# Transposing two token tiles with one transfer in a fused attention and token-mixer block

## The chip, the cores and the metric

The kernel runs on one core of a Trainium2 chip. The metric is the device time of one execution in microseconds, as the median over runs. A core has TensorE (PE) for matmuls, VectorE (DVE), ScalarE (ACT) and GpSimd (POOL) for elementwise work, and SyncE (SP), which here issues nearly all DMA transfers, one after the other in its queue.

## The reference

A block with adaptive layer norm, 2,048 tokens of 512 features, in bfloat16. The first half is attention in which each token sees 8 tokens at a distance of 2, with 32 heads of 16; the second half is an MLP over the token axis.

```python
mod = (silu(c) @ w_mod).reshape(1, 6, 1, 512)          # sa, ca, ga, sb, cb, gb
h = layernorm(x) * (1 + ca) + sa
qkv = h @ wqkv                                         # 512 -> 3 x 512, 32 heads of 16
logits = q . k[pos - 2 * w], w = 0..7                  # masked where pos - 2 w < 0
o = softmax(logits / 4) weighted sum of v
x = x + ga * (o @ wo)
h = layernorm(x) * (1 + cb) + sb
u = gelu(einsum('bsd,sf->bdf', layernorm(h), w1) + b1) # contracts the tokens, F = 1792
x = x + gb * (einsum('bdf,fs->bds', u, w2) + b2).T
```

## The kernel before

The 2,048 tokens are 16 tiles of 128. They are worked in five chunks of 2, 4, 4, 4 and 2 tiles (`SIZES`), numbered 0 to 4; chunk 2 has tiles 6 to 9, chunk 3 has 10 to 13, chunk 4 has 14 and 15. Each chunk goes through `build_chunk`:

- layer norm of its tiles: `ln1s` (statistics), `rstd1`, `nb1`, and `n1_T`, which writes the normalized tile T into `h3`, tokens on the partitions;
- a transpose of `h3` into `hT`, features on the partitions. Chunks 0 and 1 do it on TensorE (`tr`, evicted by `hT`). Chunks 2 to 4 (`XDMA`) do it by DMA: `xtT` transposes tile T, 128 tokens by 512 features, into four blocks of 128 by 128. `hT` there is laid out as feature block, then token: block k of tile T lies C columns after block k − 1, where C is the number of tokens of the chunk;
- the projections `qkvC_tj` (t = 0 for q, 1 for k, 2 for v): four matmuls each that read `hT` as the moving operand, up to 512 columns, and accumulate over the four feature blocks; evicted to `q_sb`, `k_f` and `v_sb` by `evC_tj`;
- `vdC_d`, DMA copies of shifted values from `v_sb` into a slot of `vD` (five slots);
- `qk` (VectorE products of q with shifted k into `big`), `red` (TensorE sums them into the logits `psL`), `max`, `sub`, `exp`, `esum`, `rcp`, and `smB`, which scales the weights in `lsb` on VectorE;
- `a2_C_j`, four DMA copies that lay `lsb` out anew as `a2sb`; then `pv` (VectorE products of `a2sb` and `vD` into `big`), `pvacc` (TensorE), `oev`, and the output projection `wo`;
- the second and third layer norms, which write `h3` again for the MLP.

The MLP's first matmuls (`mlp1`) take tokens as they come ready and are mixed into the chunks' work; the second ones (`mlp2`) come at the end, when all `gelu` are done. Products of `w_mod` (`modcol`, `mcols`, `mrowt`, `mrows`, `st_row`, `ld_row`) give the modulation rows; `modcol3` uses the last three loads of `w_mod` (`ld_wmod3` to `ld_wmod5`).

The order of all steps is written out by hand in the string `ORDER`, and every engine works its steps in that order. SyncE's queue is one of these orders. A DMA holds SyncE while it is issued, and the data land later; a step that waits for something holds all that stands behind it on its engine. `hT` has two buffers, so chunk 2 overwrites chunk 0's, chunk 3 chunk 1's, and chunk 4 chunk 2's. A helper records every instruction, so the profile gives line 133 for all of them, and they are told apart by their tiles: `hT<-h` are the transposing DMAs, `psS<-hT,w_qkv` the projections, `a2sb<-lsb` the `a2` copies, `vD<-v_sb` the `vd` copies.

On SyncE the steps stand in this order around the transposes, before the change: `ld_wo1 xt6 ld_wmod5 vd0_1 vd0_0 xt8 xt9 xt7 vd0_2`, the four `a2_0`, `ld_wo3 ld_wo2 xt10 ld_wo0 vd0_3 xt12 xt13 xt11 vd1_2 ld_b2`, the four `a2_1`, `vd1_1 st_row0 vd1_3 xt14 ld_row0 vd1_0 vd2_2 xt15`, and then the `a2_2` among other loads.

Of the kernel before, what the change touches and what calls it, by code (L numbers as in the profile page):

```python
# [182 lines left out]
consts ld_x_1_2 act_table ld_x0 ld_x_1_4 ld_c ld_x_2_8 ld_x1 ident ld_x_2_6 ld_wmod1 ln1s3 halo0 ld_wqkv1 cps
ln1s2 warm2 ld_wqkv0 silu_exp ld_wmod0 ln1s0 ln1s4 ln1s1 ln1s5 rstd1_0 ld_x_4_14 nb1_0 ln1s9 rstd1_1 n1_0 n1_1
silu_dve nb1_1 ld_wqkv2 ln1s8 fill:2:70 tr0_0 n1_2 n1_4 modcols1 ln1s7 hT0_3:a n1_5 n1_3 ld_x_3_10 hT0_2:d a1col
hT0_0:a fill:4:16 tr1_2 wsc1_2:d ld_b1 hT0_1:a wsc1_3:d wsc1_0:a tr1_0 wsc1_1:d ln1s6 hT1_2:a ld_wmod2 qkv0_10
ld_x_3_12 wsc0_0:d rstd1_2 wsc0_1:d qkv0_12 wsc0_2:d hT1_1:a nb1_2 n1_8 n1_9 wsc0_3:d modcols0 hT1_0:d ld_wmod3
hT1_3:a qkv0_00 sab ev0_12:d n1_6 ld_wmod4 qvb0 ln1s14 ld_wo1 qkv0_02 qvb_cp0 ln1s15 ev0_00:a wsc2_2 qvb1
wsc2_0:d qkv1_00 wsc2_3 ev0_10:a ev0_02:d ln1s10 wsc2_1:d qkv1_10 qvb_cp1 qk0_0 ev1_10:a qkv0_22 qk0_1 n1_7
qkv0_20 ln1s13 qk0_2 qkv1_02 xt6 red0_0 ev1_00:a qk0_3 red0_1 red0_2 ev0_22:a ld_wmod5 qkv1_22 qk1_0 ev0_20:a  # L190
qkv1_12 ev1_02:a vd0_1 red0_3 ev1_12:a mask qkv1_11 vd0_0 ln1s11 max0 xt8 qk1_2 qkv1_01 ev1_11:a sub0 qkv1_03
ev1_01:a xt9 exp0 qkv1_13 qk1_1 ev1_03:a xt7 esum0 ev1_13:a qkv1_20 rcp0 vd0_2 ln1s12 qkv1_21 smB0 qk1_3 a2_0_3
modcol2 rstd1_4 qkv1_23 a2_0_0 ev1_22:a a2_0_2 halo_v1:a red1_0 ev1_20:a a2_0_1 red1_1 ln1v10 ln1v12 ln1v11
ln1v13 nb1_4 red1_2 rstd1_3 n1_15 ld_wo3 red1_3 nb1_3 ld_wo2 mcols0 n1_11 n1_10 qkv2_00 max1 ev1_21:a n1_14 xt10
qkv2_02 ev2_00:a pv0_0 qkv2_10 n1_12 ld_wo0 pv0_1 qkv2_11 vd0_3 ev2_10:a ev2_02:a qkv2_12 qk2_0 n1_13 qkv2_01
xt12 ev2_12:a pvacc0_0 ev2_01:a sub1 qk2_2 xt13 qkv2_03 exp1 qkv2_13 xt11 ev2_11:a ev2_03:a qkv2_22 qk2_1
ev2_13:a esum1 ev1_23:a qkv2_21 rcp1 vd1_2 red2_0 smB1 ev2_21:a ld_b2 red2_1 qk2_3 halo_v2:a a2_1_1 red2_2
# [5 lines left out]
ld_w1_0_0 oev1_3:a mrowt1 qkv3_03 mrows1:a x1_0 st_row1 qkv4_00 ev3_03:a vd2_0 ln2q1 qk3_2 pvacc1_0 ev4_02:a
red3_1 pvacc1_1 oev1_0:a qkv3_23:q oev1_1:a qk3_3 ev4_00:a wo3:q ln2q0 wo5:q pv2_2 qkv4_22:q x1_5 ev3_23:a wo2:q
ld_row1 ln2q5 ld_w1_0_896 ln2m0 halo_v3:a wo4:q x1_3 pv2_1 x1_2 red3_2 x1_4 red3_3 ln2q3 qkv3_21:q pv2_3 rstd2_0
qkv4_20 ln2q2 ev3_21:a ev4_22:a vd3_3 pvacc2_1 nb2_0 max3 pvacc2_2 n2_0 warm0 ln2q4 vd3_0 n2_1 ln2m2 sub3 pv2_0
pvacc2_3 oev2_2:a exp3 rstd2_2 esum3 oev2_1:a aff0 pvacc2_0 rcp3 oev2_0:a qkv4_10 oev2_3:a ln2m4 nb2_2 smB3
warm3 n2_2 ev4_10:a ln3s0 wo6 a2_3_0 n2_3 ln3s1 a2_3_1 rstd2_4 wo7 x1_6 vd3_1 aff2 rstd3_0 a2_3_2 biascols wo9:q
ev4_20:a a2_3_3 nb2_4 nb3_0 ln3s3 n2_5 n2_4 vd3_2 warm1 ln3s2 h3_1 h3_0 qkv4_12 aff4 rstd3_2 wo8 x1_7 ld_w2_0
nb3_2 ln3s5 h3_3 h3_2 ln2q6 ln3s4 mlp1_0_6_0 ev4_12:a pv3_0 mlp1_0_3_0 x1_9 rstd3_4 mlp1_0_5_0 x1_8 mlp1_0_0_0  # L210
biascols_cp:a ln2q8 nb3_4 pv3_1 halo_v4:a mlp1_0_2_0 h3_4 vd4_1 h3_5 mlp1_0_1_0 ln2q9 pv3_2 ld_w2_1 mlp1_0_2_4
vd4_2 ln2q7 mlp1_0_0_4 vd4_0 mlp1_0_3_4 park0_0:a mlp1_0_1_4 mlp1_0_5_4:q park0_1:a ln2m6 vd4_3 pv3_3 park0_2:a
pvacc3_0 pvacc3_1 oev3_0:a ld_w1_0_1152 pvacc3_2 oev3_1:a mlp1_0_4_0:q rstd2_6 oev3_2:a qk4_2 pvacc3_3 park0_3:a
mlp1_0_7_0 oev3_3:a nb2_6 qk4_1 n2_6 mlp1_0_6_4 mlp1_0_4_4 n2_8 qk4_0 wo12:q ld_w1_0_1408 n2_7 n2_9 qk4_3 wo10:q
park0_4:a aff6 x1_12 red4_0 wo13:q ld_w2_3 park0_5:a ln2q12 red4_1 red4_2 x1_10 red4_3 wo11:q max4 ln2q10 ln3s9
x1_13 sub4:q mlp1_0_8_0:q exp4 ln3s8 ln2q13 mlp1_0_11_0 esum4 ln3s7 rcp4 mlp1_0_12_0 park0_6:a ln3s6 x1_11
mlp1_0_10_0 smB4 rstd3_6 ln2m12 a2_4_2 mlp1_0_9_0 h3_7 rstd2_12 h3_6 a2_4_3 ln2q11 h3_9 mlp1_0_8_4 ln2m13 a2_4_0
nb2_12 ln2m11 n2_12 mlp1_0_7_4 a2_4_1 ln2m10 h3_8 rstd2_10 ld_w2_4 aff12 mlp1_0_9_4 rstd2_13 rstd2_11 nb2_10
ln3s12 mlp1_0_9_8 mlp1_0_7_8 n2_10 mlp1_0_8_8 nb2_13 pv4_0 park0_7:a mlp1_0_12_4 ld_w1_0_1664 park0_8:a
mlp1_0_11_4 nb2_11 pv4_2 n2_13 mlp1_0_10_4 rstd3_12 pv4_1 park0_9:a mlp1_0_12_8 n2_11 mlp1_0_10_8 pv4_3 inj1_4  # L220
mlp1_0_11_8 ld_w1_1_0 park0_10:a pvacc4_2 ld_w1_1_640 park0_11:a pvacc4_0 nb3_12 aff11 pvacc4_1 h3_12 pvacc4_3
mlp1_0_13_0 aff10 oev4_0:a oev4_2:a aff13 mlp1_0_13_4 ln3s10 wo15 ld_w2_5 ln3s13 rstd3_10 mlp1_0_13_8 wo14 x1_15
rstd3_13 park0_12:a inj1_0 nb3_13 ln2s15 mlp1_1_0_6 nb3_10 x1_14 rstd2_15 mlp1_1_4_6 park0_13:a nb2_15 ln2s14
n2_15 inj1_3 inj1_6 ld_w1_1_896 inj1_5 mlp1_1_6_6 rstd2_14 aff15 h3_10 mlp1_1_3_6 ln3s15 mlp1_1_6_10 ln3s11
mlp1_1_0_10 rstd3_15 inj1_1 mlp1_1_1_6 park1_0:a nb3_15 h3_15 n2_14 rstd3_11 aff14 mlp1_1_5_6 h3_13 ln3s14
mlp1_1_5_10 mlp1_1_1_10 inj1_2 ld_w1_2_0 mlp1_1_2_6 h3_11 rstd3_14 park1_1:a h3_14 mlp1_1_4_10 mlp1_1_3_10
mlp1_1_2_10 mlp1_1_9_10 park1_2:a ld_w1_1_1408 park1_3:d mlp1_1_7_10 padd1_9 park1_4:a park1_5:d mlp1_1_8_10
padd1_7 gelu7 mlp1_1_10_10 park1_6:a mlp1_2_2_11 ld_w1_2_640 padd1_10 mlp1_2_2_14 mlp1_2_0_11 padd2_2
mlp1_2_0_14 ld_w2_7 gelu2 mlp1_2_1_11 padd2_0 mlp1_2_1_14 gelu0 mlp1_1_12_10 padd2_1 gelu10 padd1_8 gelu1
mlp1_2_5_11 gelu8 mlp1_2_5_14 gelu9 mlp1_2_6_11 mlp1_2_3_11 padd2_6 mlp1_2_3_14 ld_w2_9 mlp1_2_4_11 padd2_3  # L230
mlp1_2_4_14 padd1_12 gelu3 mlp1_1_13_10 padd2_4 gelu6 padd2_5 gelu4 mlp1_1_11_10 padd1_13 gelu5 gelu13 mlp2_0_0
padd1_11 gelu12 gelu11 mlp2_0_0b ld_w2_11 mlp2_0_0c fin0_0 mlp2_8_0 ld_w2_15 mlp2_4_0 st_out0_0 ld_w2_2 mlp2_9_0
fin4_0 ld_w2_13 mlp2_1_0 st_out4_0 mlp2_3_0 mlp2_6_0 fin3_0 fin1_0 st_out3_0 mlp2_5_0 st_out1_0 fin5_0 mlp2_7_0
st_out5_0 fin8_0 mlp2_2_0 fin9_0 mlp2_13_0 fin2_0 st_out9_0 st_out8_0 st_out2_0 fin7_0 mlp2_10_0 fin13_0
st_out7_0 fin6_0 mlp2_12_0 st_out6_0 st_out13_0 mlp2_11_0 fin12_0 fin10_0 st_out12_0 mlp2_14_0 st_out10_0
fin11_0 st_out11_0 mlp2_15_0 fin14_0 mlp2_15_1 st_out14_0 fin15_0 mlp2_15_2 fin15_1 st_out15_0 st_out15_1
fin15_2 st_out15_2
"""


# [798 lines left out]
```

## Time and profile before

| | |
|---|---|
| time, median of 3 runs | 206.31 us (206.3 to 206.35) |
| profiled execution, first to last instruction | 204.6 us |
| the run's median less that span | 1.7 us |
| TensorE busy | 194.7 us, 95% of the span |
| VectorE busy | 163.3 us, 80% |
| ScalarE busy | 120.6 us, 59% |
| GpSimd busy | 13.0 us, 6% |
| mean granted TensorE clock | 0.998 |
| transposing DMAs | 10, from 22.2 to 57.0 us |

Times inside the profile count from the span's first instruction. "Busy" counts neither waiting nor the issuing of DMAs; SyncE's issues are shown in its timeline as SPq. A matmul's row has its full latency, so matmuls that follow each other overlap; the rate is read from the distance of their starts. A busy share is an average: the stretches of the execution have different limits.

### The profile page before, as it was taken

The page shows a single profiled execution, that of the slowest core. Times are in us where ns is not written, and L with a number is a line of the kernel's source. Part 1 is how long each engine was busy: PE and PEld are TensorE (multiplying, and loading weights), DVE is VectorE, ACT ScalarE, POOL GpSimd, SP SyncE. Part 2 cuts the span into 40 slices and gives each one's busy share as a digit, 9 for nine tenths or more (in the row PEclk, how much of TensorE's full clock was granted, in tenths as well). Part 3 has the DMA queues.
Part 4 walks back from the last instruction along what each step waited for, and adds up shares of the span by engine and source line. Part 5 has one row for each costly group of instructions (what it writes and reads, how often), then busy time and mean ns, then how long its engine had stood idle before and what let it go on. Part 6 is the DMA issues. An engine that isn't in the chain of part 4 may idle for free.

```text
span 204.6 us, 4223 instructions
## 1 busy us (share of the span) xinstructions
PE 194.7 (95%) x1655; PEld 103.5 (51%) x1655; DVE 163.3 (80%) x260; ACT 120.6 (59%) x283; POOL 13.0 (6%) x36
## 2 busy tenths in 40 slices
PE   3999999999999997989899999999999999999994
PEld 3988554454455553554344445444444444444453
DVE  2899999999999999999999999975473204369365
ACT  2398998994666899989898876683762000000000
POOL 4122001100000001240000000100000000000000
...
GB/s 141 330 380 348 117 239 107 161 98 201 247 186 267 308 234 251 25 272 110 289 200 115 26 157 263 288 131 200 340 304 3 232 88 16 39 77 51 51 82 51
DMA packets 55111, 35.93 MB, mean 176 GB/s; under 512 B 24628, under 2 KB 52404, under 8 KB 55092
## 3 DMA queue, kind: packets, MB, share of 16 engines
...
q10 hardware_dynamic: 8, 0.00, 0.0%
...
## 4 chain that ended last, share of the span: by engine, by line
PE 65%; DVE 20%; issue 5%; DMA 5%; SPq 3%; ACT 2%; DVEq 0%
PE psS L133 62%; DVE big L133 9%; DVE h L133 3%; PE psL L133 3%; SPq L133 3%; DVE st L133 3%; DMA wst<-in_B_w_dram 2%; DMA xx<-in_A_x_dram 2%; ACT h L133 1%; DVE mv L133 1%; DVE m L133 1%; DVE lsb L133 1%; DVE ls L133 0%; DVE nb L133 0%; DVE woq L133 0%
## 5 line engine op out<-in xcount | busy, mean ns | idle before, releaser
L133 PE MATMUL psS<-h,wst 128*128 128x512 bf16 (+1 forms) x254 | 50.7, 379 | 1.2 <-POOL h L133 0.7
L133 PE MATMUL psS<-hT,w_qkv 128*128 128x512 bf16 (+3 forms) x312 | 46.2, 339 | 0.3 <-ACT w_qkv L133 0.3
L133 PEld LDWEIGHTS <-wst 128*128 128x128 bf16 (+1 forms) x356 | 28.7, 98 | 32.2 <-issue 3.2
L133 PEld LDWEIGHTS <-w_qkv 128*128 128x128 bf16 (+1 forms) x354 | 29.5, 111 | 21.3 <-issue 3.2
L133 DVE TENSOR_TENSOR big<-a2sb,vD 128x4096 bf16<-128x4096 bf16 (+1 forms) x20 | 36.9, 1876 | 0.0
L133 DVE TENSOR_TENSOR big<-q_sb,k_f 128x4096 bf16<-128x4096 bf16 (+1 forms) x20 | 36.3, 1857 | 0.0
L133 DVE SCALAR_TENSOR_TENSOR h<-psS,bcol,rows_bc 128x512 f32<-128x512 f32 (+2 forms) x18 | 12.4, 690 | 24.4 <-PE psS L133 24.2
L133 PE MATMUL psS<-gT,big 128*128 128x512 bf16 x112 | 24.8, 379 | 0.0
L133 PEld LDWEIGHTS <-big 128*128 128x128 bf16 x144 | 12.0, 97 | 13.2
L133 PEld LDWEIGHTS <-ident 128*128 128x128 bf16 (+1 forms) x203 | 13.9, 111 | 5.9 <-issue 2.8
L133 PE MATMUL psS<-woq,o_sb 128*32 128x512 bf16 (+1 forms) x172 | 16.6, 380 | 0.0
L133 ACT ACTIVATE h<-xx,nb,rs 128x512 bf16<-128x512 bf16 x19 | 15.0, 807 | 0.8 <-DVE nb L133 0.7
L133 DVE TENSOR_TENSOR psS<-psS,gT 128x512 f32<-128x512 f32 x14 | 9.3, 696 | 7.0 <-PE psS L133 7.0
L133 ACT ACTIVATE junk<-xx 128x512 bf16<-128x512 bf16 x22 | 13.8, 626 | 0.2
L133 POOL TENSOR_SCALAR h<-xx,rs,nb 128x512 bf16<-128x512 bf16 x9 | 7.3, 813 | 101.3 <-DVE nb L133 84.0
L133 ACT ACTIVATE lv<-mv,epscol 128x1 f32<-128x1 f32 (+2 forms) x25 | 7.3, 291 | 9.3 <-DVE mv L133 8.4
L133 DVE BATCH_NORM_STATS2 st<-xx 128x6 f32<-128x512 bf16 x14 | 9.5, 678 | 4.0 <-DMA xx<-in_A_x_dram 4.0
L133 ACT ACTIVATE gT<-psS,bcol 128x512 bf16<-128x512 f32 x14 | 8.7, 688 | 6.4 <-DVE psS L133 6.4
L133 PEld LDWEIGHTS <-group 128*32 128x32 bf16 x288 | 6.8, 96 | 10.2 <-issue 4.8
L133 DVE TENSOR_TENSOR h<-h,rows_bc 128x512 bf16<-128x512 bf16 (+2 forms) x20 | 11.5, 581 | 0.5
L133 DVE TENSOR_TENSOR h<-h,xx 128x512 bf16<-128x512 f32 (+2 forms) x18 | 11.4, 633 | 0.6
L133 ACT ACTIVATE gT<-psS 128x512 bf16<-128x512 f32 x19 | 10.8, 587 | 1.6 <-PE psS L133 1.5
...
## 6 DMA issues: line engine op xcount, KB each, us to landing
...
```

What stands on the lines that cost most here:

```text
L133: r = fn(*a, **k)
```

## The change

A parameter `XG=2` is added. In chunks 2 to 4 one transposing DMA handles two tiles: the source is 128 tokens by 2 x 512 columns of `h3`, and the result is eight blocks of 128 by 128. `hT` of these chunks is now laid out by tile, then feature block, so that the blocks of one transfer follow each other. A projection's moving operand for feature block kt is now one piece of 128 columns from each tile of the chunk, 512 columns apart, instead of one contiguous row. Chunks 0 and 1 stay as they are. Ten transposing DMAs become five: `xt6` (tiles 6 and 7), `xt8` (8 and 9), `xt10`, `xt12` and `xt14`. In `ORDER` they stand where the chunk's last ones stood; nothing else is moved.

```diff
     XDMA=(2, 3, 4),
+    XG=2,
...
+        rhs_of = lambda kt: hT[:, kt, :]
         if ch in XDMA:
-            first = None
-            for sl, st in enumerate(tiles):
-                dma_t = lambda sl=sl, st=st: nc.sync.dma_start_transpose(out=hT[:, :, sl * P:(sl + 1) * P],
-                                                                         in_=h3[:, st, :])
-                add("sp", 1.25, dma_t, reads=[("n1", st)] + ([("hT_raw", bh)] if sl else []),
+            hX = hT_r[bh][:, 0:KT * C].rearrange("p (s k q) -> p s k q", s=nt, k=KT)
+            rhs_of = lambda kt: hX[:, :, kt, :]
+            for sl in range(0, nt, XG):
+                st = t0 + sl
+                dma_t = lambda sl=sl, st=st: nc.sync.dma_start_transpose(
+                    out=hX[:, sl:sl + XG, :, :].rearrange("p s k q -> p (s k) q"),
+                    in_=h3[:, st:st + XG, :].rearrange("p s d -> p (s d)"))
+                add("sp", 1.25, dma_t, reads=[("n1", s) for s in range(st, st + XG)] + ([("hT_raw", bh)] if sl else []),
                     writes=[("hTr", ch, sl)] + ([] if sl else [("hT_raw", bh)]), bytes_=0.95, lat=1.2, desc=8,
                     name=f"xt{st}")
-            hkeys = [("hTr", ch, sl) for sl in range(nt)]
+            hkeys = [("hTr", ch, sl) for sl in range(0, nt, XG)]
...
-                        mm(ps(s_)[:, (j - j0) * C:(j - j0 + 1) * C], lhsT=lhsT, rhs=hT[:, kt, :],
+                        mm(ps(s_)[:, (j - j0) * C:(j - j0 + 1) * C], lhsT=lhsT, rhs=rhs_of(kt),
```

SyncE's order after it: `ld_wo1 ld_wmod5 vd0_1 vd0_0 xt6 xt8 vd0_2`, the four `a2_0`, `ld_wo3 ld_wo2 ld_wo0 vd0_3 xt10 xt12 vd1_2 ld_b2`, the four `a2_1`, `vd1_1 st_row0 vd1_3 ld_row0 vd1_0 vd2_2 xt14`, and the rest as before.

More of the change, by code (lines that the diff above doesn't have):

```diff
@@ L182 @@
 ORDER = """
[L183 to L197, printed above, removed]
@@ L198 @@
-pvacc0_1 a2_1_3 qkv3_00 a2_1_2 qkv3_10 a2_1_0 pv0_2 mrowt0 vd1_1 qkv2_20 ev3_10:a pv0_3 ev3_00:a red2_3 mrows0:a
-qkv2_23 ev2_20:a st_row0 max2 halo_k3:p ev2_22:a vd1_3 qkv3_11 qk3_0 xt14 qkv3_22 ev3_11:a pvacc0_2 ld_row0
-pvacc0_3 sub2:q oev0_2:a vd1_0 pv1_2 qkv3_02:q exp2 qkv3_12 ev3_02:a ev2_23:a qkv3_01 pv1_3 oev0_0:a vd2_2 esum2
-modcol3 xt15 rcp2 ev3_12:a woq_s qkv3_20 ev3_01:a pvacc1_3 smB2 ev3_20:a red3_0 qk3_1 ev3_22:a a2_2_0 pvacc1_2
-wo1 a2_2_1 vd2_3 qkv3_13:q x1_1 a2_2_2 pv1_1 vd2_1 wo0 ev3_13:a a2_2_3 qkv4_02 ld_w1_0_512 oev1_2:a mcols1 pv1_0
@@ L203 @@
[L203 to L237, printed above, removed]
+consts ld_x_1_2 act_table ld_x0 ld_x_1_4 ld_c ld_x_2_8 ld_x1 ident ld_x_2_6 ld_wmod1 ln1s3 halo0 ld_wqkv1 cps ln1s2
@@ new lines @@
+warm2 ld_wqkv0 silu_exp ld_wmod0 ln1s0 ln1s4 ln1s1 ln1s5 rstd1_0 ld_x_4_14 nb1_0 ln1s9 rstd1_1 n1_0 n1_1 silu_dve
+nb1_1 ld_wqkv2 ln1s8 fill:2:70 tr0_0 n1_2 n1_4 modcols1 ln1s7 hT0_3:a n1_5 n1_3 ld_x_3_10 hT0_2:d a1col hT0_0:a
+fill:4:16 tr1_2 wsc1_2:d ld_b1 hT0_1:a wsc1_3:d wsc1_0:a tr1_0 wsc1_1:d ln1s6 hT1_2:a ld_wmod2 qkv0_10 ld_x_3_12
+wsc0_0:d rstd1_2 wsc0_1:d qkv0_12 wsc0_2:d hT1_1:a nb1_2 n1_8 n1_9 wsc0_3:d modcols0 hT1_0:d ld_wmod3 hT1_3:a qkv0_00
+sab ev0_12:d n1_6 ld_wmod4 qvb0 ln1s14 ld_wo1 qkv0_02 qvb_cp0 ln1s15 ev0_00:a wsc2_2 qvb1 wsc2_0:d qkv1_00 wsc2_3
@@ new lines @@
+ev0_10:a ev0_02:d ln1s10 wsc2_1:d qkv1_10 qvb_cp1 qk0_0 ev1_10:a qkv0_22 qk0_1 n1_7 qkv0_20 ln1s13 qk0_2 qkv1_02
+red0_0 ev1_00:a qk0_3 red0_1 red0_2 ev0_22:a ld_wmod5 qkv1_22 qk1_0 ev0_20:a qkv1_12 ev1_02:a vd0_1 red0_3 ev1_12:a
+mask qkv1_11 vd0_0 ln1s11 max0 qk1_2 qkv1_01 ev1_11:a sub0 qkv1_03 ev1_01:a exp0 qkv1_13 qk1_1 ev1_03:a xt6 xt8 esum0
+ev1_13:a qkv1_20 rcp0 vd0_2 ln1s12 qkv1_21 smB0 qk1_3 a2_0_3 modcol2 rstd1_4 qkv1_23 a2_0_0 ev1_22:a a2_0_2 halo_v1:a
+red1_0 ev1_20:a a2_0_1 red1_1 ln1v10 ln1v12 ln1v11 ln1v13 nb1_4 red1_2 rstd1_3 n1_15 ld_wo3 red1_3 nb1_3 ld_wo2 mcols0
@@ new lines @@
+n1_11 n1_10 qkv2_00 max1 ev1_21:a n1_14 qkv2_02 ev2_00:a pv0_0 qkv2_10 n1_12 ld_wo0 pv0_1 qkv2_11 vd0_3 ev2_10:a
+ev2_02:a qkv2_12 qk2_0 n1_13 qkv2_01 ev2_12:a pvacc0_0 ev2_01:a sub1 qk2_2 qkv2_03 exp1 qkv2_13 xt10 xt12 ev2_11:a
+ev2_03:a qkv2_22 qk2_1 ev2_13:a esum1 ev1_23:a qkv2_21 rcp1 vd1_2 red2_0 smB1 ev2_21:a ld_b2 red2_1 qk2_3 halo_v2:a
+a2_1_1 red2_2 pvacc0_1 a2_1_3 qkv3_00 a2_1_2 qkv3_10 a2_1_0 pv0_2 mrowt0 vd1_1 qkv2_20 ev3_10:a pv0_3 ev3_00:a red2_3
+mrows0:a qkv2_23 ev2_20:a st_row0 max2 halo_k3:p ev2_22:a vd1_3 qkv3_11 qk3_0 qkv3_22 ev3_11:a pvacc0_2 ld_row0
@@ new lines @@
+pvacc0_3 sub2:q oev0_2:a vd1_0 pv1_2 qkv3_02:q exp2 qkv3_12 ev3_02:a ev2_23:a qkv3_01 pv1_3 oev0_0:a vd2_2 esum2
+modcol3 xt14 rcp2 ev3_12:a woq_s qkv3_20 ev3_01:a pvacc1_3 smB2 ev3_20:a red3_0 qk3_1 ev3_22:a a2_2_0 pvacc1_2 wo1
+a2_2_1 vd2_3 qkv3_13:q x1_1 a2_2_2 pv1_1 vd2_1 wo0 ev3_13:a a2_2_3 qkv4_02 ld_w1_0_512 oev1_2:a mcols1 pv1_0 ld_w1_0_0
+oev1_3:a mrowt1 qkv3_03 mrows1:a x1_0 st_row1 qkv4_00 ev3_03:a vd2_0 ln2q1 qk3_2 pvacc1_0 ev4_02:a red3_1 pvacc1_1
+oev1_0:a qkv3_23:q oev1_1:a qk3_3 ev4_00:a wo3:q ln2q0 wo5:q pv2_2 qkv4_22:q x1_5 ev3_23:a wo2:q ld_row1 ln2q5
@@ new lines @@
+ld_w1_0_896 ln2m0 halo_v3:a wo4:q x1_3 pv2_1 x1_2 red3_2 x1_4 red3_3 ln2q3 qkv3_21:q pv2_3 rstd2_0 qkv4_20 ln2q2
+ev3_21:a ev4_22:a vd3_3 pvacc2_1 nb2_0 max3 pvacc2_2 n2_0 warm0 ln2q4 vd3_0 n2_1 ln2m2 sub3 pv2_0 pvacc2_3 oev2_2:a
+exp3 rstd2_2 esum3 oev2_1:a aff0 pvacc2_0 rcp3 oev2_0:a qkv4_10 oev2_3:a ln2m4 nb2_2 smB3 warm3 n2_2 ev4_10:a ln3s0
+wo6 a2_3_0 n2_3 ln3s1 a2_3_1 rstd2_4 wo7 x1_6 vd3_1 aff2 rstd3_0 a2_3_2 biascols wo9:q ev4_20:a a2_3_3 nb2_4 nb3_0
+ln3s3 n2_5 n2_4 vd3_2 warm1 ln3s2 h3_1 h3_0 qkv4_12 aff4 rstd3_2 wo8 x1_7 ld_w2_0 nb3_2 ln3s5 h3_3 h3_2 ln2q6 ln3s4
@@ new lines @@
+mlp1_0_6_0 ev4_12:a pv3_0 mlp1_0_3_0 x1_9 rstd3_4 mlp1_0_5_0 x1_8 mlp1_0_0_0 biascols_cp:a ln2q8 nb3_4 pv3_1 halo_v4:a
+mlp1_0_2_0 h3_4 vd4_1 h3_5 mlp1_0_1_0 ln2q9 pv3_2 ld_w2_1 mlp1_0_2_4 vd4_2 ln2q7 mlp1_0_0_4 vd4_0 mlp1_0_3_4 park0_0:a
+mlp1_0_1_4 mlp1_0_5_4:q park0_1:a ln2m6 vd4_3 pv3_3 park0_2:a pvacc3_0 pvacc3_1 oev3_0:a ld_w1_0_1152 pvacc3_2
+oev3_1:a mlp1_0_4_0:q rstd2_6 oev3_2:a qk4_2 pvacc3_3 park0_3:a mlp1_0_7_0 oev3_3:a nb2_6 qk4_1 n2_6 mlp1_0_6_4
+mlp1_0_4_4 n2_8 qk4_0 wo12:q ld_w1_0_1408 n2_7 n2_9 qk4_3 wo10:q park0_4:a aff6 x1_12 red4_0 wo13:q ld_w2_3 park0_5:a
@@ new lines @@
+ln2q12 red4_1 red4_2 x1_10 red4_3 wo11:q max4 ln2q10 ln3s9 x1_13 sub4:q mlp1_0_8_0:q exp4 ln3s8 ln2q13 mlp1_0_11_0
+esum4 ln3s7 rcp4 mlp1_0_12_0 park0_6:a ln3s6 x1_11 mlp1_0_10_0 smB4 rstd3_6 ln2m12 a2_4_2 mlp1_0_9_0 h3_7 rstd2_12
+h3_6 a2_4_3 ln2q11 h3_9 mlp1_0_8_4 ln2m13 a2_4_0 nb2_12 ln2m11 n2_12 mlp1_0_7_4 a2_4_1 ln2m10 h3_8 rstd2_10 ld_w2_4
+aff12 mlp1_0_9_4 rstd2_13 rstd2_11 nb2_10 ln3s12 mlp1_0_9_8 mlp1_0_7_8 n2_10 mlp1_0_8_8 nb2_13 pv4_0 park0_7:a
+mlp1_0_12_4 ld_w1_0_1664 park0_8:a mlp1_0_11_4 nb2_11 pv4_2 n2_13 mlp1_0_10_4 rstd3_12 pv4_1 park0_9:a mlp1_0_12_8
@@ new lines @@
+n2_11 mlp1_0_10_8 pv4_3 inj1_4 mlp1_0_11_8 ld_w1_1_0 park0_10:a pvacc4_2 ld_w1_1_640 park0_11:a pvacc4_0 nb3_12 aff11
+pvacc4_1 h3_12 pvacc4_3 mlp1_0_13_0 aff10 oev4_0:a oev4_2:a aff13 mlp1_0_13_4 ln3s10 wo15 ld_w2_5 ln3s13 rstd3_10
+mlp1_0_13_8 wo14 x1_15 rstd3_13 park0_12:a inj1_0 nb3_13 ln2s15 mlp1_1_0_6 nb3_10 x1_14 rstd2_15 mlp1_1_4_6 park0_13:a
+nb2_15 ln2s14 n2_15 inj1_3 inj1_6 ld_w1_1_896 inj1_5 mlp1_1_6_6 rstd2_14 aff15 h3_10 mlp1_1_3_6 ln3s15 mlp1_1_6_10
+ln3s11 mlp1_1_0_10 rstd3_15 inj1_1 mlp1_1_1_6 park1_0:a nb3_15 h3_15 n2_14 rstd3_11 aff14 mlp1_1_5_6 h3_13 ln3s14
@@ new lines @@
+mlp1_1_5_10 mlp1_1_1_10 inj1_2 ld_w1_2_0 mlp1_1_2_6 h3_11 rstd3_14 park1_1:a h3_14 mlp1_1_4_10 mlp1_1_3_10 mlp1_1_2_10
+mlp1_1_9_10 park1_2:a ld_w1_1_1408 park1_3:d mlp1_1_7_10 padd1_9 park1_4:a park1_5:d mlp1_1_8_10 padd1_7 gelu7
+mlp1_1_10_10 park1_6:a mlp1_2_2_11 ld_w1_2_640 padd1_10 mlp1_2_2_14 mlp1_2_0_11 padd2_2 mlp1_2_0_14 ld_w2_7 gelu2
+mlp1_2_1_11 padd2_0 mlp1_2_1_14 gelu0 mlp1_1_12_10 padd2_1 gelu10 padd1_8 gelu1 mlp1_2_5_11 gelu8 mlp1_2_5_14 gelu9
+mlp1_2_6_11 mlp1_2_3_11 padd2_6 mlp1_2_3_14 ld_w2_9 mlp1_2_4_11 padd2_3 mlp1_2_4_14 padd1_12 gelu3 mlp1_1_13_10
@@ new lines @@
+padd2_4 gelu6 padd2_5 gelu4 mlp1_1_11_10 padd1_13 gelu5 gelu13 mlp2_0_0 padd1_11 gelu12 gelu11 mlp2_0_0b ld_w2_11
+mlp2_0_0c fin0_0 mlp2_8_0 ld_w2_15 mlp2_4_0 st_out0_0 ld_w2_2 mlp2_9_0 fin4_0 ld_w2_13 mlp2_1_0 st_out4_0 mlp2_3_0
+mlp2_6_0 fin3_0 fin1_0 st_out3_0 mlp2_5_0 st_out1_0 fin5_0 mlp2_7_0 st_out5_0 fin8_0 mlp2_2_0 fin9_0 mlp2_13_0 fin2_0
+st_out9_0 st_out8_0 st_out2_0 fin7_0 mlp2_10_0 fin13_0 st_out7_0 fin6_0 mlp2_12_0 st_out6_0 st_out13_0 mlp2_11_0
+fin12_0 fin10_0 st_out12_0 mlp2_14_0 st_out10_0 fin11_0 st_out11_0 mlp2_15_0 fin14_0 mlp2_15_1 st_out14_0 fin15_0
@@ L238 @@
+mlp2_15_2 fin15_1 st_out15_0 st_out15_1 fin15_2 st_out15_2
 """
```

## The prediction

> **What bounds the kernel now.** I read the busy time by stretch first, cut where the chain of waits changes engine: TensorE until 57, VectorE to 113, TensorE to the end.
>
> ```profile
> core 0: us, PE busy (x) PEld busy (x) DVE busy (x) ACT busy (x) POOL busy (x), PEclk, DMA share, GB/s
> 13.60:57.00 43.40, 43.39 (x395) 24.69 (x396) 43.11 (x52) 36.10 (x78) 3.41 (x5) 1.00 0.73 200
> 57.00:75.00 18.00, 17.91 (x293) 10.09 (x294) 17.86 (x14) 13.68 (x36) 0.00 (x0) 1.00 0.77 242
> 75.00:112.80 37.80, 34.37 (x378) 17.00 (x371) 37.08 (x55) 35.16 (x92) 4.22 (x5) 1.00 0.67 183
> 112.80:201.60 88.80, 88.74 (x465) 41.83 (x464) 55.45 (x112) 29.39 (x66) 0.77 (x1) 1.00 0.49 137
> ```
>
> VectorE idles 0.29, 0.14 and 0.72 us in the first three stretches: 1.15 us in 99. TensorE has slack only from 75 to 112.8 (3.4 us), where it waits for VectorE. From 112.8 on TensorE streams without a break. So a microsecond put on VectorE before 112.8 is a microsecond at the end, and a wait removed elsewhere brings nothing unless VectorE had been idle for it. The changed transfers all lie between 22 and 59 us.
>
> Next, SyncE's own timeline where chunk 2's four transposes (tiles 6, 8, 9, 7) are issued. Columns: start, duration, what, count.
>
> ```profile
> 22.21 1.31 SPq L133 DMA_TRANSPOSE hT<-h  x1
> 23.57 0.56 SPq L133 DMA_DIRECT2D gT<-in_w_mod_dram  x1
> 25.30 1.27 SPq L133 DMA_DIRECT2D vD<-v_sb  x2
> 26.69 3.93 SPq L133 DMA_TRANSPOSE hT<-h  x3
> 30.66 0.59 SPq L133 DMA_DIRECT2D vD<-v_sb  x1
> 31.70 2.65 SPq L133 DMA_DIRECT2D a2sb<-lsb  x4
> ```
>
> A transpose holds the queue 1.3 us, twice a plain copy. Behind the transposes wait `vd0_2` and the four `a2_0` copies; the latter start at 31.70, just after VectorE's `smB0` (`lsb`, done at 31.67), not when the queue comes free at 31.25. Who needs these, from VectorE's timeline, and what GpSimd does beside it:
>
> ```profile
> 35.15 1.21 DVE L133 TENSOR_REDUCE m<-psL 128x128 bf16<-128x1024 f32 x1
> 36.28 2.71 DVE L133 TENSOR_TENSOR big<-a2sb,vD 128x2048 bf16<-128x2048 bf16 x2
> 38.91 6.68 DVE L133 TENSOR_TENSOR big<-q_sb,k_f 128x4096 bf16<-128x4096 bf16 x3
> ...
> 35.26 1.52 POOL L133 TENSOR_SCALAR h<-xx,rs,nb 128x512 bf16<-128x512 bf16 x2 [17.31 <-DVE mcols L133]
> ```
>
> The two products `big<-a2sb,vD` at 36.28 are `pv0_0` and `pv0_1`, the first users of `a2_0`. Landing times are in the answers for tiles hT and a2sb:
>
> ```profile
> L133 SPq DMA_TRANSPOSE hT<-h x10: 1211/1285/1714, 22.2 to 57.0; - x10
> DMA to landing us min/median/max: 2.6/3.5/4.7
> ...
> L133 SPq DMA_DIRECT2D a2sb<-lsb x20: 609/629/894, 31.7 to 115.7; - x20
> DMA to landing us min/median/max: 2.0/2.1/3.1
> ```
>
> **The change, part by part.** *Issue cost of a pair (D).* No two-tile transpose is in the trace. From below: 1.21 us, the shortest single one. From above: 3.43 us, twice the longest. What grows with the tile is 1.285 less the fixed part of an issue; plain issues take 0.28 us (a copy to scratch, 1 KB) to 0.63 us (a2). So the growing part is 0.65 to 1.0 us and D is 1.9 to 2.3; I take 2.05. [...]
>
> *Chunk 2's queue.* `xt6` leaves its place at 22.21, so the `w_mod` load behind it goes up from 23.57 to about 16.9; its user, `modcol3`, runs at 57. The two `vD` copies stay at 25.30, held by `v_sb`. Then pair 1 runs from 26.69 to 28.74 and pair 2 to 30.83, `vd0_2` to 31.5, and `a2_0` starts at 31.70 as before: no slip, with 0.2 us to spare. In general the slip of `a2_0` is 2 x (D − 2.15). The last of the four starts at 33.72 (31.70 + 2.65 − 0.63) and lands 2.0 to 2.1 later, at 35.8; VectorE takes it up at 36.28. So 0.5 us more is covered, by `max1` (35.15 to 36.36), and the cover ends at D = 2.4. [...]
>
> *Chunk 2's landing.* A single transpose lands 3.5 − 1.29 = 2.2 us after its issue ends. With up to 1.3 us more for the second tile, pair 2 lands between 33.0 and 34.3. TensorE takes up chunk 2's projections at 35.01 (the PE rows below), so 0.7 us remain at worst.
>
> *Chunks 3 and 4.* `ld_wo0` and `vd0_3` go up past `xt10` on SP. `xt10` then starts near 37 and `xt12` when the last of chunk 3's normalized tiles is there, 39.7 on ScalarE, ending near 41.8; the last single transpose ended at 42.99, and the next issue waits for `v_sb` until 44.47. Chunk 3's first projection is at 46.84. In chunk 4 the pair starts where `xt15` did, 57.03. `xt15` took 1.63, so with 0.65 to 1.0 more it ends by 59.7, before `a2_2` at 60.21, which waits for VectorE. It lands by 62.9 against 63.98, when chunk 4's projections begin. The row load ahead of it, at 52.73, moves up half a microsecond; its user `woq_s` at 58.37 follows a busy VectorE (53.96 + 4.48 = 58.44) and gains nothing. All nought.
>
> *Projections in pieces of 128.* The PE timeline has a moving operand read in pieces, the correction with the maximum: at 27.89 it reads eight pieces of 64.
>
> ```profile
> 27.89 0.38 PE L133 MATMUL psL<-m,nident 128*128 128x512 bf16 x1
> 28.11 1.89 PE L133 MATMUL psS<-hT,w_qkv 128*128 128x512 bf16 x8
> ...
> 35.01 1.27 PE L133 MATMUL psS<-hT,w_qkv 128*128 128x512 bf16 x5
> ```
>
> Its successor starts 0.22 us later. Contiguous projections follow each other at (1.89 − 0.38)/7 = 0.216. So pieces cost nothing that shows; rounding allows 0.01 us on some 120 matmuls of 512 columns (96 in chunks 2 and 3, and 48 of half width), 1.2 us on a full TensorE. These pieces repeat one row, though, and the changed ones step 1 KB. I take 0 and keep 1.2 for the range.
>
> *Sum.* 0 on VectorE, 0 on TensorE. SyncE saves some 14.0 − 10.3 = 3.7 us of issuing (ten singles of 1.4 against five of 2.05), which nobody waits for. Span 204.6 as now; what lies around it is 206.3 − 204.6 = 1.7 us; the time stays at 206.3.
>
> **The rivals.**
>
> *Slower: a pair costs more than two singles and holds `a2_0`.* Place: the SP queue from 26.69 to 31.7. It decides above D = 2.4. For it: chunk 2's pairs now stand together, where one of the four singles used to be out of the way at 22.21, and three singles elsewhere took 1.5 to 1.7 us. Against: in this very place they took 1.31 at most. At twice the median, D = 2.57, `a2_0` slips 0.8 and VectorE 0.3 us. At D = 3, `a2_0` slips 1.7, VectorE 1.2: 207.5. At D = 3.43 it is 2.1 us, 208.4, and pair 2 then lands after 35.01 too. That the pair is carried out as two transposes after all is the D = 2.57 case: 206.6. 0.31.
>
> *Slower: strided pieces slow the moving read.* Up to 1.2 us, 207.5. Against: the row above. 0.07.
>
> *Faster: SP's relief reaches VectorE.* It can win only the idle time that VectorE has, 0.29 + 0.14 until 75: 205.9, or 205.2 if the 0.72 after 75 went too. Against: no VectorE row from 33 to 46 has a wait in brackets, and the gaps between rows are under 0.1 us. 0.16.
>
> **How the numbers follow.** No change, 206.3, has 0.46. The bound is 0.2%, 0.4 us, about what a measurement of this kernel can tell from no change. Slower takes the two slower rivals, 0.38, faster 0.16. The likeliest case's own range is 205.9 to 206.7. The range goes down to 205.8, VectorE's idle time before 75 and a little, and up to 207.7, which takes in D to 3 and the pieces, and leaves out D above 3.1 and the idle time after 75.
>
> **What would show it.** Right: five DMA_TRANSPOSE rows of 1.9 to 2.3 us; `a2sb<-lsb` again at 31.7; `pv0_0` at 36.3; projections 0.216 us apart; VectorE's busy share before 112.8 as now; TensorE's last stretch starting at 112.8. Wrong: `a2_0` past 32.3 with an idle VectorE before `pv0_0` (the first rival); projections further apart (the second); the last stretch starting before 112.4 (the third), above all with VectorE instructions shorter, which nothing here foresees.

## The result: slower by 0.35%

| | before | after |
|---|---|---|
| time, median of 20 runs each, on one chip | 207.19 us (206.29 to 208.02) | 207.81 us (206.44 to 208.3) |
| ratio, 95% interval | | 1.0035 [1.0018, 1.0051] |
| profiled execution | 206.3 us, span 204.6 | 207.49 us, span 205.5 |

The kernel before scatters too: over all series on record here, 160 runs of it have a median of 206.95, and 82 of them lie below 207.0. The 206.31 shown ahead of the prediction was three runs from the low end: of the 1.5 us from there to 207.81, 0.9 lie in the kernel before itself (207.19) and 0.6 in the change. Of the changed kernel's 20 runs, 2 lie below 207.0, of the 20 of before beside them 9. That count is given with the runs below; a part of the scatter turns out to have a cause. One run below, of the singles in the pairs' place, took 289.84 us at a granted clock of 0.662 and is in no ratio.

### The profile page after: what moved, and what is told of

It is laid out like the page before. It is cut to its first block, busy times and chain, and to the rows that moved or that the text cites. A ratio compares the mean times of both kernels' runs of the same rounds, so it can differ in the third digit from the quotient of the medians.

```text
span 205.5 us, 4211 instructions
## 1 busy us (share of the span) xinstructions
PE 194.3 (95%) x1655; PEld 102.9 (50%) x1655; DVE 163.1 (79%) x260; ACT 120.5 (59%) x283; POOL 13.0 (6%) x36
## 4 chain that ended last, share of the span: by engine, by line
PE 47%; DVE 32%; issue 9%; ACT 5%; DMA 4%; SPq 2%; DVEq 0%
PE psS L133 47%; DVE big L133 22%; DVE h L133 3%; DVE st L133 3%; SPq L133 2%; DMA xx<-in_A_x_dram 2%; ACT h L133 2%; DMA woq<-in_A_wo_dram 2%; DVE lsb L133 1%; DVE mv L133 1%; DVE m L133 1%; ACT v_sb L133 1%; ACT junk L133 1%; ACT q_sb L133 1%; DVE ls L133 0%
## 5 line engine op out<-in xcount | busy, mean ns | idle before, releaser
L133 PE MATMUL psS<-woq,o_sb 128*32 128x512 bf16 (+1 forms) x172 | 16.6, 380 | 0.0
L133 PEld LDWEIGHTS <-ident 128*128 128x128 bf16 (+1 forms) x203 | 13.3, 109 | 6.0 <-issue 2.9
L133 ACT ACTIVATE k_f<-psS 128x512 bf16<-128x512 f32 x15 | 8.9, 593 | 5.5 <-PE psS L133 5.5
```

The source lines that it names most:

```text
L133: r = fn(*a, **k)
```

## The profile after, beside that of before

VectorE's and TensorE's busy time by stretch, cut where it was cut before:

```profile
core 0: us, PE busy (x) PEld busy (x) DVE busy (x) ACT busy (x) POOL busy (x), PEclk, DMA share, GB/s
13.60:57.00 43.40, 42.49 (x387) 23.92 (x386) 42.02 (x51) 35.16 (x78) 3.41 (x5) 1.00 0.70 198
57.00:75.00 18.00, 17.90 (x286) 10.20 (x287) 17.86 (x14) 13.59 (x36) 0.00 (x0) 1.00 0.74 232
75.00:112.80 37.80, 34.85 (x390) 17.26 (x379) 37.12 (x53) 35.17 (x92) 4.22 (x5) 1.00 0.70 191
```

Only the first stretch differs: VectorE idles 1.38 us there (43.40 − 42.02), where it idled 0.29. SyncE's queue in that stretch (start, duration, what, count):

```profile
26.33 2.83 SPq L133 DMA_TRANSPOSE hT<-h  x2
29.21 0.69 SPq L133 DMA_DIRECT2D vD<-v_sb  x1
31.45 2.65 SPq L133 DMA_DIRECT2D a2sb<-lsb  x4
34.15 2.81 SPq L133 DMA_DIRECT2D woq<-in_A_wo_dram  x3
```

Two pairs take 2.83 us of the queue, `vd0_2` is out at 29.9, and the `a2_0` copies start at 31.45, behind `smB0` as before and 0.25 us earlier than then. The queue isn't what holds them. VectorE, though, waits for them:

```profile
34.90 1.21 DVE L133 TENSOR_REDUCE m<-psL 128x128 bf16<-128x1024 f32 x1
37.24 2.36 DVE L133 TENSOR_TENSOR big<-a2sb,vD 128x2048 bf16<-128x2048 bf16 x2 [1.12 <-DMA woq<-in_A_wo_dram]
39.51 6.69 DVE L133 TENSOR_TENSOR big<-q_sb,k_f 128x4096 bf16<-128x4096 bf16 x3
```

`max1` ends at 36.11 and `pv0_0` starts 1.12 us later. The bracket names the `wo` load that landed nearest in time; what `pv0_0` needs is `a2_0`, as the landing times in the answers for tiles hT and a2sb show (the first cut to 14 to 62 us, since later two loads of weights go into tiles of the same name):

```profile
L133 SPq DMA_TRANSPOSE hT<-h x5: 1231/1313/1717, 26.3 to 57.7; - x5
...
DMA to landing us min/median/max: 3.3/3.9/5.7
...
L133 SPq DMA_DIRECT2D a2sb<-lsb x20: 609/628/1212, 31.5 to 116.3; - x20
DMA to landing us min/median/max: 2.0/2.2/3.5
```

The last `a2_0` copy, issued at 33.49, is the one that took 3.5 us: it landed at 37.02 instead of about 35.6. What else was in the DMA engines is in the DMA view of the stretch from 34 to 35.2 us, first of before, then of after (queue, kind: packets, MB, share of 16 engines):

```profile
q1 hardware_dynamic: 435, 0.05, 27.1%
```

```profile
GB/s 0 0 0 34 43 55 94 119 149 154 141 107 73 51 34 21 13 4 0 0 0 0 0 546 0 43 38 55 98 102 137 158 137 90 47 47 43 17 13 0
...
q1 hardware_dynamic: 527, 0.06, 33.0%
q8 instruction: 1, 0.02, 6.2%
...
a2sb<-lsb SPq DMA_DIRECT2D x1, 32.0 KB, 3.5
```

A packet of q8, of the kind "instruction", is there, 16 KB in one piece; the GB/s line cuts the 1.2 us into 40 slices, and the 546 at 34.7 us is its start. 6.2% of 16 engines over 1.2 us are 1.19 us of one engine, and the packet took 1.20 by the kept trace: the worth of one DMA engine for all that time. The page's part 3 has 13 of them in the whole execution, in both kernels:

```profile
q8 instruction: 13, 0.21, 0.4%
```

In before, this fetch comes at 35.35 us, and the last packets of `a2_0` were through at 35.41. In after it comes at 34.72, and the last packets of `a2_0` are through only at 36.16. The kept trace also has the steps of the semaphore that counts a copy's landing, 16 for each copy. For the last `a2_0` copy of before all 16 came from 35.50 to 35.76. In after 15 came from 35.24 to 35.51 and the sixteenth at 37.02: one step of sixteen was held, while the fetch had the worth of one engine of sixteen. The trace doesn't name the engine of a packet; that it is the same one is concluded from these times. TensorE was at almost the same place of its stream both times: 357 of its weight loads had started ahead of the fetch in before, 356 in after.

The second difference is at the end: VectorE's last rows, with the span in the first line of each answer, before and then after.

```profile
core 0 of [0], span 204.6 us
...
201.99 0.29 DVE L133 TENSOR_TENSOR h<-h,xx 128x128 bf16<-128x128 f32 x1
```

```profile
core 0 of [0], span 205.5 us
...
202.59 0.29 DVE L133 TENSOR_TENSOR h<-h,xx 128x128 bf16<-128x128 f32 x1
```

From the end of VectorE's last instruction to the end of the span (unrounded 204.57 and 205.51) it is 2.29 us before and 2.63 after.

The account of the profiled pair, +0.94 us: `max1` starts 0.25 earlier (34.90 against 35.15; the first projection had already started 0.35 earlier, with an earlier landing of the first loads). From `max1` to `qk2_0` it is 4.61 us against 3.76, +0.85: the wait of 1.12, less what `pv0_0` and `pv0_1` gain (2.36 against 2.71), and 0.08 by which `pv0_0` had started ahead of the end of `max1`'s row in before. That leaves VectorE 0.60 late, and 0.60 it stays: TensorE's last stretch starts at 113.43 instead of 112.83, and VectorE's last row at 202.59 instead of 201.99. The end adds 0.33.

## The experiments

The theories, as the expectations name them. **F**: an instruction fetch falls on the last `a2_0` copy and holds it; when the fetch comes is set by TensorE's instruction stream, and the change only shifted the one against the other. **L**: at the end, SyncE waits for the DMAs' completion semaphores. The program has eight, and the DMAs take them in turn; SyncE waits for them in one fixed order (in both kernels S102 first, S108 last). Before, the last store signals S108, the semaphore that is waited for last; with five DMAs fewer it signals S102, the one that is waited for first, and the other waits come on top. (The kept traces have these waits: before, the last store lands at 203.74 and the last wait ends at 203.79; after, it lands at 204.36, the wait for it ends at 204.40, and five more end by 204.71.) **Q**, the rival: it is the pairs themselves, their place in the queue or their longer transfers, that hold `a2_0`. Each kernel has 12 runs, beside 23 or 35 of the kernel before in the same series. The steps `fill:N:M` are matmuls of no result that fill waits; `:q` behind a projection has its matmuls issued in four pieces of 32 output features, so TensorE has more instructions for the same work.

**The kernel before once more.** No edit.

> The kernel before, unchanged, to see what its spread consists of (206.3 to 208.0 us in 20 runs). Theory F (a 16 KB instruction fetch of TensorE, queue q8 of the page, falls on the last a2_0 copy and holds its last packets): runs fall in two groups, near 206.3 without and near 207.3 to 207.9 with the collision, and a profile of a run above 207 us shows an idle VectorE of about 1 us before pv0_0 (36 to 38 us) and the fetch at or before 35.2; one below 206.7 shows none. Rival Q (the paired transposes crowd the DMA queue ahead of a2_0): the kernel before has no pairs, so its profile never shows that idle time, whatever its time.

206.79 us, 7 of 12 below 207.0, ratio 1.0005 [0.9983, 1.0026]. Its profiled execution took 207.48, and VectorE's timeline shows the wait of after, in the kernel before:

```profile
35.64 1.22 DVE L133 TENSOR_REDUCE m<-psL 128x128 bf16<-128x1024 f32 x1
37.42 2.36 DVE L133 TENSOR_TENSOR big<-a2sb,vD 128x2048 bf16<-128x2048 bf16 x2 [0.56 <-DMA a2sb<-lsb]
```

The fetch came at 34.63, the issue of `a2_0` ended at 34.85, its last packets were through at 36.52; 15 of the last copy's 16 steps came by 36.26, the sixteenth at 37.30. So the wait needs no pair, and the kernel before has it in one of its two profiled executions. It is not the whole scatter of before, though. This execution's span is 0.92 us longer than the first profile's, and 0.49 of that stands at `max1` already (35.64 against 35.15), ahead of the collision: TensorE, and VectorE behind it, had waited for a late load of `w_mod`.

```profile
15.88 0.55 PE L133 MATMUL psS<-sc,big 128*128 128x1 bf16 x16 [0.84 <-DMA big<-in_w_mod_dram]
```

From `max1` to `qk2_0` the collision adds 0.30 (4.06 us against 3.76).

**Before, the fetch earlier.**

```diff
-esum0 ev1_13:a qkv1_20 rcp0
+esum0 ev1_13:a qkv1_20:q rcp0
```

> The kernel before with one projection step ahead of the spot (qkv1_20) issued as four matmuls of 32 columns each: same TensorE time, 24 more instructions, so the instruction fetch comes at an earlier point of TensorE's program, about 0.7 us earlier, near 34.6 instead of 35.35, onto the last a2_0 copies. F: VectorE idles 0.5 to 1.2 us before pv0_0 and the kernel takes 207.2 to 208, as the changed one does, in nearly every run. Q and rival P (pieces of 128 columns slow the projections): no change, spread as before, some runs at 206.3.

206.54 us, 9 of 12 below 207.0, ratio 0.998 [0.9962, 0.9998]. The expectation was a miss: the fetch moved by 2.1 us, to 33.27, not by 0.7, and fell on the earlier copies instead of the last one. The second copy landed 3.3 us after its issue (15 of 16 steps by 34.23, the sixteenth at 35.55), and the four copies held the queue for 3.39 us instead of 2.65:

```profile
31.49 3.39 SPq L133 DMA_DIRECT2D a2sb<-lsb  x4
```

All four were in by 36.29, though; `pv0_0` waits 0.04 us, and the kernel is a little faster. Run again in another series:

> e2 again, on the chip of e9 to e11, as their measure: 206.2 to 207.2, median 206.5, 0.2% below the kernel before, 2.3 us end, no idle VectorE before pv0_0.

206.75, 11 of 12 below 207.0, 0.9988 [0.997, 1.0007]. The wait was not expected, but it is there: with the fetch at 33.68 the last copy was in at 36.46, and VectorE idles 0.41 us ahead of `pv0_0`. The earlier fetch makes the wait shorter, not always nought.

**Before and after without a filler.** Meant to move the fetch later.

```diff
-fill:4:16 tr1_2
+tr1_2
```

> The kernel before without the same 16 fillers. F: 206.0 to 206.6 us in every run, the slow group gone, and equal to the changed kernel without fillers within 0.2%, so the change itself costs nothing. Q or P: the changed kernel without fillers stays 0.7 us above this one.

> The changed kernel without the 16 filler matmuls at about 11 us (32 TensorE instructions less, no work of the result). The fetch then comes 32 instructions later in the program, where TensorE issues some 9 a microsecond: near 38 us, behind the a2_0 copies. F: no idle VectorE before pv0_0, last a2_0 copy lands 2.1 us after its issue, 206.0 to 206.6 us. Q and P: 207.5 to 208 as the changed kernel, a2_0 lands late as before.

Before: 206.72, 7 of 12, ratio 1.0000 [0.9977, 1.0023], fetch at 35.36, no collision in the profile, and the scatter still there. After: 207.69, 2 of 12, 1.0034 [1.0013, 1.0054], fetch at 35.02, `a2_0` landing at 37.32, VectorE idle 1.25 us. Both are misses: this fetch did not move, or by 0.3 us, so these runs decide nothing on F. Others of the 13 did (the eighth of the changed kernel from 94.14 to 100.59), with nothing edited but TensorE's stream.

**After, the fetch earlier.** The edit of the second experiment on the changed kernel.

> The changed kernel with the step that e2 has (qkv1_20 as four matmuls of 32 columns each, 24 more TensorE instructions of the same time). In e2 this brought the fetch from 35.35 to 33.27, ahead of the last copies. F: the fetch comes near 33, the last a2_0 copy is in by 36.3, VectorE idles under 0.2 us before pv0_0, and the kernel takes 206.2 to 206.7 in most runs: the change itself costs nothing. Q or P: 207.5 to 208, 0.5% above e2's 206.5.

206.96 us, 8 of 12 below 207.0, ratio 1.0006 [0.9985, 1.0027]. The fetch is at 33.47, and VectorE doesn't wait (its row, and the DMA view from 33 to 34.5 us):

```profile
36.49 2.47 DVE L133 TENSOR_TENSOR big<-a2sb,vD 128x2048 bf16<-128x2048 bf16 x2
```

```profile
q8 instruction: 1, 0.02, 4.0%
```

With the pairs in place and only TensorE's stream lengthened, 0.0029 of the 0.0035 are gone by the medians, which speaks for F and against Q. The same edit had made the kernel before faster too, and that has the collision in one of its two profiles; so the two ratios, of F undone and of L undone, need not add up to the loss. The end still takes 2.63. Against the kernel with singles and the same step in the same series (the new layout alone, below: 206.49) 0.47 us are left, of which the end is 0.33.

**After, the fetch much earlier.** `qkv1_13`, `qkv1_20` and `qkv1_21` all in pieces.

> The changed kernel with three projection steps so split (72 more TensorE instructions, qkv1_20, qkv1_21, qkv1_13). F: the fetch comes before 32, ahead of all a2_0 copies (32.5 to 35.2), the last one lands 2.1 us after its issue, 206.2 to 206.6 us and fewer slow runs than e5. Q or P: 207.5 to 208.

207.29 us, 2 of 12, ratio 1.0015 [0.9995, 1.0034]. The fetch at 31.52 frees `pv0_0`, but all later fetches moved as well, and one now falls on chunk 4's copies, `a2_4`:

```profile
118.79 1.23 DVE L133 TENSOR_TENSOR big<-a2sb,vD 128x2048 bf16<-128x2048 bf16 x1 [0.65 <-DMA a2sb<-lsb]
```

Of that copy's 16 steps 15 came by 116.80 and the last at 118.54. VectorE isn't the bound there, but TensorE comes to wait for it:

```profile
123.54 0.40 PE L133 MATMUL psS<-big,group 128*32 128x256 bf16 x8 [0.33 <-DVE big L133]
```

From the start of TensorE's last stretch to the end of VectorE's last row it takes 90.17 us here, against 89.45 both before and after. So the fetch that was moved off one copy costs 0.7 us at another, and the time says nothing against F. The end takes 2.61.

**Before, the fetch a little earlier.**

```diff
-fill:4:16 tr1_2
+fill:4:20 tr1_2
```

> The kernel before with 20 instead of 16 filler matmuls at about 11 us (8 more TensorE instructions). F: the fetch comes some 0.2 to 0.4 us earlier, from 35.35 to about 35.0, into the window in which the last a2_0 packets are still to go (until 35.4): VectorE idles about 1 us before pv0_0 and most runs take 207.2 to 208, without any pair. Q: as the kernel before, about half of the runs below 206.7.

Profiled execution 207.51: fetch at 35.16, last packets of `a2_0` at 36.63, and the wait, with single transposes:

```profile
37.54 2.36 DVE L133 TENSOR_TENSOR big<-a2sb,vD 128x2048 bf16<-128x2048 bf16 x2 [0.99 <-DMA a2sb<-lsb]
```

In time, 207.08, 4 of 12, 1.0006 [0.9986, 1.0026]: the direction, but nothing that can be told from no change.

**The new layout alone.** Before's order with singles (`XG=1`), `hT` by tile and then block, projections in pieces of 128; with `qkv1_20:q`, so that it stands against the second experiment.

> The kernel before with ten single transposes in their old places, but the new layout by tile, so that the projections read pieces of 128 columns; with e2's step, so that the fetch is out of the way. P: 0.3 to 1.2 us above e2, projections further apart than 0.216 us. F and Q: e2's time, 206.2 to 206.7, projections 0.216 us apart.

206.49 us, 12 of 12 below 207.0, ratio 0.9967 [0.9946, 0.9988]: the fastest kernel here, ahead of both. Its interval overlaps that of the second experiment, so nothing shows that the pieces gain anything. TensorE's row of the first 24 matmuls of chunk 2's projections, before and then with pieces:

```profile
35.01 5.37 PE L133 MATMUL psS<-hT,w_qkv 128*128 128x512 bf16 x24
```

```profile
35.04 5.37 PE L133 MATMUL psS<-hT,w_qkv 128*128 128x512 bf16 x24
```

**The end.** Loads of 4 KB that nobody uses, put behind `st_out4_0`, turn the order of the semaphores: five give back what the change took, three more than before's give after's place.

```diff
-st_out4_0 mlp2_3_0
+st_out4_0 pad0 pad1 pad2 pad3 pad4 mlp2_3_0
```

After, fetch earlier, and five pads:

> e5 plus five small unused loads (4 KB each) on SyncE at about 164 us, where its queue is idle, so that the number of DMAs is again that of the kernel before. Theory L (the end): DMAs take eight completion semaphores in turn, SyncE at the end waits for them in a fixed order (S102 first, S108 last); with five DMAs fewer the last store signals S102, and the five waits after it, some 0.06 us each, come on top: 2.62 us from VectorE's last instruction to the end of the span instead of 2.30, in all four profiles with pairs so far against 2.29 to 2.32 in the six without. L: 2.3 us here, and 0.3 us below e5: 206.2 to 206.7, median as e12. If the 0.3 us are the final store's own delay: 2.6 us and e5's 207.0.

206.98 us, 6 of 12 below 207.0, in a series where before had 207.20 and 14 of 35, ratio 0.9994 [0.9977, 1.0012]. With both causes undone the loss against before is gone, and the pairs are all in place. The fairer measure is the kernel before with the same earlier fetch, 206.75 in this series: against it 0.23 us are left, which the runs (206.31 to 207.36 and 206.24 to 207.16) can't tell from nothing. The end of VectorE's timeline (span unrounded 204.63):

```profile
core 0 of [0], span 204.6 us
...
202.02 0.29 DVE L133 TENSOR_TENSOR h<-h,xx 128x128 bf16<-128x128 f32 x1
```

2.31 us, before's distance. Before, fetch earlier, and three pads:

> e2 (no pairs) plus three such loads at the same place: the last store then signals S102 as in the changed kernel. L: 2.62 us from VectorE's last instruction to the end, 0.3 us above e12: 206.5 to 207.0. Without L: 2.3 us and e12's time.

```profile
core 0 of [0], span 204.6 us
...
201.69 0.29 DVE L133 TENSOR_TENSOR h<-h,xx 128x128 bf16<-128x128 f32 x1
```

204.59 − 201.98 = 2.61 us, after's distance, with not a transpose changed; 207.19 us, 4 of 12, a little above what was expected, and 1.0004 [0.9979, 1.003], against 206.75 for the same kernel without pads in the same series. After with the five pads alone:

> The changed kernel plus the five loads, its fetch left where it is. L with F: 0.3 us below the changed kernel (207.81), near 207.5, with a 2.3 us end, but an idle VectorE of about 1 us before pv0_0 as before in most runs. L alone as the whole cause: the kernel before's distribution, half of the runs below 206.8.

207.37 us, 1 of 12, ratio 1.0022 [1.0003, 1.0042]: the end takes 2.30, the wait ahead of `pv0_0` stays (1.54 us; fetch at 35.18, `a2_0` landing at 37.76). The distance takes only these two values in all profiles here: 2.61 to 2.63 where the last store's semaphore is waited for first, 2.29 to 2.32 where last.

**Singles in the pairs' place.** The kernel before with all four transposes of chunk 2 where the two pairs stand.

```diff
-qkv1_02 xt6 red0_0 ... max0 xt8 qk1_2 ... ev1_01:a xt9 exp0 ... ev1_03:a xt7 esum0
+qkv1_02 red0_0 ... max0 qk1_2 ... ev1_01:a exp0 ... ev1_03:a xt6 xt7 xt8 xt9 esum0
```

> The kernel before with chunk 2's four single transposes standing together where the changed kernel has its two pairs (after the vD copies); everything else as before. This is the place without the pairing, and the forecast's slower rival at twice a single's issue: queue occupied from 26.7 to 31.9, a2_0 first issued near 32.6 instead of 31.7, last copy in near 36.7, VectorE 0.3 us late at least, more where the fetch also falls on the copies: 206.9 to 208. If the queue does not matter (transposes issued back to back overlap): a2_0 at 31.7 and the kernel before's distribution.

207.56 us, 0 of 12, ratio 1.0028 [1.0007, 1.005]. SyncE's queue:

```profile
26.35 5.27 SPq L133 DMA_TRANSPOSE hT<-h  x4
31.66 0.59 SPq L133 DMA_DIRECT2D vD<-v_sb  x1
32.36 2.67 SPq L133 DMA_DIRECT2D a2sb<-lsb  x4
```

Here the queue itself is late: four issues of 1.32 us push `a2_0` to 32.36, 0.9 us behind after's 31.45, and VectorE idles 1.25 us. It is the slip that the prediction feared of the pairs; two pairs hold the queue for 2.83 us and spare it. The fetch, at 34.81, meets the late copies as well (last packets at 36.54): 15 of the last copy's steps came by 36.43, the sixteenth at 37.31, and `pv0_0` starts 0.12 us after that. Without the fetch the slip alone would have cost some 0.4 us, an estimate from these steps (36.43 + 0.12, less the end of `max1` at 36.18); the rest of the 1.25 is the fetch.

**The first pair back at its early place**, with the five pads, against the run with pads alone.

> e11 (changed kernel, five small loads at the end) with chunk 2's first pair back at the early place of xt6, ahead of the w_mod load, about 22 us. If the later place and the earlier w_mod load are what puts the fetch on the a2_0 copies in nearly every run: the kernel before's distribution, median 206.8, fetch 1.0 us or more after the last a2_0 issue ends is no rarity, VectorE without idle time. If the place is not it: e11's distribution, median 207.4, with about 1 us idle before pv0_0.

207.21 us, 5 of 12, ratio 1.0015 [0.9993, 1.0037]; in its profile the fetch is at 33.81 and the wait 0.45. That execution was the fastest of the twelve all the same, 206.17, since its work had come to `max1` early, at 34.57: again the wait is not the whole scatter. The median lies between, and its interval holds both no loss and the whole of what was left. It doesn't settle whether the place of the first pair makes the collision more frequent.

## Why the prediction was wrong

The forecast of no change fell; slower by 0.35% came out, 207.81 us, 0.1 above the range. That the number left the range is owed more to the 206.31 it started from than to the change, since the kernel before took 207.19 beside it. What the forecast had wrong is the 0.6 us between the two. Point by point:

- **The bound**: right. VectorE's 0.60 us before 112.8 arrived whole at TensorE's last stretch and at the end.
- **The term D, the issue of a pair**: mis-sized. I took 2.05 us, from the reasoning that the part of an issue that grows with the tile doubles. Pairs took 1.23 to 1.72, median 1.313, where singles took 1.21 to 1.71, median 1.285: next to nothing grows at the queue. The second tile shows in the landing: 3.9 us in the median instead of 3.5. SyncE saves 13.7 − 7.0 = 6.7 us of issuing instead of 3.7, and nobody waits for it, as forecast.
- **The slip of `a2_0` in the queue**: none, as forecast, and with more than the 0.2 us to spare.
- **The step that failed**: the last `a2_0` copy "lands 2.0 to 2.1 later, at 35.8", and on that rested "So 0.5 us more is covered, by `max1`". It started at 33.49 and landed 3.5 later, since an instruction fetch held a sixteenth of it: VectorE waited 1.12 us, and 0.85 arrived. As the time of an undisturbed copy the term was right, and the maximum of 3.1 us in the quoted line was no sign: it comes from the copies of 64 KB in the other chunks. The DMA view of before tells the two sizes apart (median to landing in the last column), and its four `a2_0` copies took 2.0 to 2.1.

```profile
a2sb<-lsb SPq DMA_DIRECT2D x12, 64.0 KB, 2.2
...
a2sb<-lsb SPq DMA_DIRECT2D x8, 32.0 KB, 2.0
```

The sign was a fetch at 35.35, just as the last packets of this very copy were in work (through at 35.41), and the prediction has no rival with a transfer of another queue on the copy. Its price could have been worked out: 16.6% of 16 engines from 35 to 35.5 us are 1.33 us of one engine, less the cover of 0.5 some 0.8 us of VectorE, an estimate near what came. The DMA view of before from 35 to 35.5 us has it:

```profile
q8 instruction: 1, 0.02, 16.6%
```

- **The slower rival** had the place (`a2_0`, VectorE idle before `pv0_0`) and the wrong mechanism: D above 2.4. With four singles in the pairs' place `a2_0` does slip in the queue; with the pairs it doesn't.
- **The price of a slip ahead of `pv0_0`**: the prediction lets a slip cost in full beyond the 0.5 us that `max1` covers, which is up to 0.35 us too much. In before `pv0_0` starts at 36.28, while GpSimd runs until 36.78, and takes 1.57 us; in after GpSimd is done at 36.54, `pv0_0` starts at 37.24 and takes 1.22. And where it starts while GpSimd still runs, it was longer by what GpSimd had left less 0.13 to 0.15 us: 0.36 of 0.50 us (before), 0.18 of 0.32 (after, the fetch much earlier), 0.12 of 0.27 (after, the fetch earlier), 0.08 of 0.22 (the new layout alone), 0.01 of 0.14 (before, the fetch earlier). So a later start wins back a part of the slip.
- **The pieces of 128**: cost nothing, as forecast; 5.37 us for 24 matmuls either way.
- **The sum's last term**: "what lies around it" and the end were taken as unchanged. The end grew by 0.33 us, because fewer DMAs put the last store on another semaphore. No view of before spoke of it but the sequence of semaphore waits at the end, which I had not read.

What is shown: the loss has two parts, and with both undone it is gone against before with the pairs kept (0.9994; 0.1% above before with the same earlier fetch). The end has 0.33 us, about half of the 0.62 between the medians. What the collision costs an execution is shown too. That the rest of the loss is the fetch meeting the copy in more executions fits the runs, but with one profile for each kernel, two for the one before, it is not shown how often it does. The kernel before has the same collision in one of its two profiles. A tenth of a microsecond of the wait stands behind the landing: where `pv0_0` waits for the last landing, it starts 0.22 us after it in the kernels with pairs, where the kept traces have two wait instructions ahead of it, and 0.12 in those without, where they have one. What stays open is how often each has it, and why the changed kernel should have it more often. The fetch came 1.0 to 1.1 us behind the end of the last `a2_0` issue where they missed each other (before, and before without the filler), 0.6 to 0.7 us behind it (after, also without the filler or with five pads) or 0.2 us ahead of it (before once more) where they met, so some 0.4 us of shift decide, an estimate from these distances. That the issue moved is seen; that it is the pairs' place which moves the two against each other was only argued, and the run meant for it was inconclusive.
